# Attention in units of two head pairs, group 0's a\*b by attention segment, batch 1 inside the weight fold

## The chip, the core and the metric

The kernel runs on one core of one Trainium2 chip. The metric is device time in microseconds (us) of one execution, as a median over runs.

## The reference

Sliding-window causal attention over 8 batches, 8 heads, 576 positions and head size 64 (each query sees itself and the 63 positions before it), followed by a multiplicative feed-forward over the 4608 tokens of width 512:

```python
scores = scale * np.matmul(q, k.transpose(0, 1, 3, 2))
mask = (rel >= 0) & (rel < 64)
attn = exp(where(mask, scores, -1e9) - max); attn = attn / (sum(attn) + 1e-9)
x = np.matmul(attn, v)          # transposed to (4608 tokens, 512)
h = (x @ w1) * (x @ w2) @ w3    # w1, w2: 512 x 1024; w3: 1024 x 1024
out = h @ w_out                 # w_out: 1024 x 512
```

## The kernel before, in words

**Numbers.** Everything is multiplied in fp16 with fp32 sums. `w3 @ w_out` is folded on the chip into one matrix `wc_sb` (1024 x 512), so that a group of tokens costs `a`, `b`, their product, and one matmul with `wc_sb`.

**Attention units.** A batch has 12 units: 3 segments of 192 queries (`SEGS`) times 4 head pairs `j`. `scores(u)` (L251) computes the scores of one head pair with two matmuls into one PSUM tile `s_ps`, takes `exp` on ACT (L264) and zeroes what lies outside the window by two `affine_select` on POOL for each group of columns (L271, L273; segment 0 has two groups, so four of them). `values(u)` (L277) multiplies with v, whose tile carries columns of ones, so that four matmuls give the output and the row sums in `o_ps`; the division is two `Ln` of the sums (L298, L299), one `exp` of minus that (L301) and two DVE multiplies into the ring `xT` (L304, L305). `s_ps` and `o_ps` have two buffers of one PSUM bank each.

**Loads.** `load_qk` brings one batch of k or q into a tile of the four-buffer pool `stage`; `cast_qk` makes fp16 halves of it; `transposes` turns six 128x128 blocks on PE into `tp` (or into a buffer of `f_ps` while `early`) and copies them to `kT` or `qT`. `load_v` is a POOL-issued DMA that casts on the way; `copy_v` (L222) makes the two shifted v blocks on DVE. The weights come through `stage` too (`load_w12`, `load_wo`, `load_w3`), and are cast by DVE or POOL.

**Feed-forward.** 9 groups of 512 tokens. `ffn_ab(g, fc)` does 8 matmuls of 512 columns into two of the three `f_ps` buffers, an ACT copy (L379) and a DVE multiply (L380). `ffn_o(g, t)` does 8 matmuls, a DVE copy (L388) and, later, a store. `fold_t(fc)` turns a row block of w3 by 8 transposes (L432) and a DVE copy (L434); `fold_mm(fc)` does 8 matmuls (L440) and an ACT copy (L441).

**Order.** The order is written out by hand; each engine executes its own instructions in that order. First comes batch 0: loads, casts, transposes, then its 12 units alone, with filler matmuls on PE (`keep_busy`, L459) between them. Then a list of `slots`: 8 `ffn_ab` of group 0 with the casts and transposes of batch 1 hung on them (`todo`, L549), 8 fold steps, 4 `ffn_o`; from there on each group is 8 `ffn_ab` and 4 `ffn_o`. Each slot has a due time in units (L566 to L568), and after a slot `tick(u)` runs the units that are due: `scores(u)`, `values(u - LAG)` with `LAG = 2`, and the loads, casts and transposes for later batches (`late`, `second`). The units of batch 1 run one after each fold step and each of the first `ffn_o`.

Of the kernel before, what the change touches and what calls it, by code (L numbers as in the profile page):

```python
# [11 lines left out]
ALU = mybir.AluOpType  # L12
# [132 lines left out]
def kernel(  # L145
# [21 lines left out]
    RING = 4 * S  # L167

# [12 lines left out]
    ps_s = fast.enter_context(tc.tile_pool(name="ps_s", bufs=2, space=PSUM))  # L181
    ps_v = fast.enter_context(tc.tile_pool(name="ps_v", bufs=2, space=PSUM))
# [68 lines left out]
    def scores(u):  # L251
        b, r = divmod(u, 12)
        si, j = divmod(r, NJ)
        kT, qT = kTs[b], qTs[b % 2]
        seg = SEGS[si]
        w = sum(blk[2] for blk in seg)
        s_ps = ps_s.tile([P, 512], FP32, name="s_ps")
        c0 = 0
        for (k0, q0, n, _) in seg:
            nc.tensor.matmul(s_ps[:, c0:c0 + 2 * n].rearrange("k (a n) -> k a n", a=2), kT[:, j, k0:k0 + P],  # L260
                             qT[:, j, :, q0:q0 + n], start=True, stop=True, skip_group_check=True)
            c0 += 2 * n
        pt = sb.tile([P, 512], FP16, name="pt", bufs=4)
        nc.scalar.activation(pt[:, 0:2 * w], s_ps[:, 0:2 * w], AF.Exp, bias=-SHIFT, scale=scale)  # L264

        c0 = 0
        groups = [(0, 256, 128, 0, 0), (256, 384, 64, 64, 0)] if si == 0 else [(0, 512, 128, 64, -64)]
        for (lo, hi, n, off, step) in groups:
            sl = pt[:, lo:hi]
            nb = (hi - lo) // (2 * n)  # L270
            nc.gpsimd.affine_select(out=sl, in_=sl, pattern=[[step, nb], [0, 2], [1, n]], compare_op=ALU.is_ge,  # L271
                                    fill=0.0, base=off, channel_multiplier=-1)
            nc.gpsimd.affine_select(out=sl, in_=sl, pattern=[[-step, nb], [0, 2], [-1, n]], compare_op=ALU.is_ge,  # L273
                                    fill=0.0, base=63 - off, channel_multiplier=1)
        probs[u] = pt

    def values(u):  # L277
        b, r = divmod(u, 12)
        si, j = divmod(r, NJ)
        v16 = v16s[b % 2]  # L280
        pt = probs.pop(u)
        seg = SEGS[si]
        q_base = seg[0][1]
        o_ps = ps_v.tile([P, 2, 192], FP32, name="o_ps")
        first = True
        for a in range(2):
            c0 = 0
            for bi, (k0, q0, n, _) in enumerate(seg):
                nc.tensor.matmul(o_ps[:, a, q0 - q_base:q0 - q_base + n],  # L289
                                 v16[:, si * 2 + bi, j, a * D:a * D + P],  # L290
                                 pt[:, c0 + a * n:c0 + a * n + n],
                                 start=first, stop=(bi == 1), skip_group_check=True)
                first = False
                c0 += 2 * n
# [10 lines left out]
        nc.vector.tensor_tensor(xs[D:P], o_ps[D:P, 1, :], r[D:P], ALU.mult)  # L305

    NU = 12 * B
    LAG = 2
    VLOADS = {3: 0, 4: 2, 5: 3, 6: 4, 7: 5}

    def keep_sums(n):
# [5 lines left out]
    late = {5: [("load", 2, "q"), ("v", 1, 3)],  # L317
# [3 lines left out]
            9: [("copy", 1, 1), ("cast", 2, "k", 1)], 11: [("copy", 1, 4)]}  # L321
    second = {3: [("v", 1, 0)], 4: [("v", 1, 2)], 5: [("v", 1, 3)], 6: [("v", 1, 4)],
# [19 lines left out]

    def tick(u):

        b, r = divmod(u, 12)
        if u < NU:
            scores(u)
        ev = [] if b == 0 else (second if b == 1 else late).get(r, [])
# [15 lines left out]
    def ffn_ab(g, fc):  # L364
        if fc == 0:
            abs_[g] = sb.tile([P, 8, GT], FP16, name="ab", bufs=3)
        ab = abs_[g]
        a_ps = ps_f.tile([P, GT], FP32, name="f_ps")
        b_ps = ps_f.tile([P, GT], FP32, name="f_ps")
        x0 = g * GT % RING  # L370
        cuts = [(0, GT)] if x0 + GT <= RING else [(0, RING - x0), (RING - x0, GT)]
        for w, d in ((w1_sb, a_ps), (w2_sb, b_ps)):
            for dc in range(4):
                for ci, (lo, hi) in enumerate(cuts):
                    xc = (x0 + lo) % RING
# [82 lines left out]

# [13 lines left out]
    vl = list(VLOADS.values())  # L472
    for i, v16 in enumerate(v16s):
        nc.gpsimd.memset(v16.rearrange("p c j (a e) -> p (c j a) e", a=2)[:, :, D:2 * D], 1.0)
        if i == 0:
            load_v(0, vl[0])
    wst = [load_w12(moe_w1, 0), load_w12(moe_w2, 0)]
    keep_busy(45)
    for which in "kq":
        cast_qk(0, which, 0, dve_cp)  # L480
        cast_qk(0, which, 1, act_cp if which == "k" else pool_cp)
        for c in range(3):
# [139 lines left out]
```

## Time and profile before

| what | value |
|---|---|
| time, median of 3 runs | 339.63 us (338.09 to 339.88) |
| the profiled execution, its own time | 336.5 us |
| span of the profiled execution | 334.8 us |
| busy: PE, DVE, ACT, POOL | 287.5, 216.5, 211.9, 207.4 us |
| mean granted TensorE clock | 0.958 |

The shares of the whole span hide that the kernel has stages with different limits. The stages as they are used below: up to 26.5 us the first loads, until the first `values`; up to 64.5 us attention of batch 0, group 0's `ffn_ab` and batch 1's transposes; up to 114.25 us the weight fold with attention of batch 1 and group 0's `ffn_o`; up to 299 us groups 1 to 7 with the rest of the attention; then the last group.

### The profile page before, as it was taken

Reading aid. Unit: us, or ns where it says so; the run is one execution under the profiler, and the core shown is the slowest. Engines: PE = TensorE matmul, PEld = TensorE weight load, DVE = VectorE, ACT = ScalarE, POOL = GpSimd, SP = SyncE. Lnnn points to the kernel's source line nnn. Section 1 sums busy time; section 2 is a strip of 40 time slices with the busy share of each in tenths; the row PEclk is TensorE's granted clock in tenths of the full one; section 3 lists DMA queues with packets and bytes.
Section 4 is the critical chain, followed back from the end, with each engine's and each line's share of the span. In section 5 each row is a group of like instructions: output and inputs, shape, how many; then the busy total and the mean of one; then the engine's idle time right before and its main releaser. Section 6 shows DMA issues by size and latency. Waiting matters only on the chain.

```text
span 334.8 us, 6342 instructions
## 1 busy us (share of the span) xinstructions
PE 287.5 (86%) x2119; PEld 173.3 (52%) x2119; DVE 216.5 (65%) x395; ACT 211.9 (63%) x493; POOL 207.4 (62%) x341
## 2 busy tenths in 40 slices
PE   5727589669766999999999999999999999997890
PEld 5716555335433555555655679655555555543340
DVE  5424758924446966797898787768977866565230
ACT  1427873457625678698898877579879977732100
POOL 8454982759955757679978955778897564300000
PEclk9786989999979999999999999999999999999597
DMA  6992889983910395568857853196077020030011
GB/s 190 364 294 8 215 124 282 413 360 42 297 18 31 114 289 34 112 201 148 120 164 184 80 143 105 25 229 89 3 131 70 0 96 33 3 114 15 2 72 65
DMA packets 52203, 44.18 MB, mean 132 GB/s; under 512 B 39312, under 2 KB 39312, under 8 KB 52160
## 3 DMA queue, kind: packets, MB, share of 16 engines
q1 hardware_dynamic: 14656, 38.95, 33.5%
q0 software_dynamic: 37504, 4.72, 22.8%
q8 instruction: 19, 0.31, 0.4%
q14 instruction: 24, 0.20, 0.2%
HBM read 38.80 MB, written 9.44 MB: 144 GB/s over the span
## 4 chain that ended last, share of the span: by engine, by line
PE 67%; DVE 9%; POOL 9%; DMA 6%; issue 3%; ACT 3%; SPq 1%; DVEq 0%; POOLq 0%; ACTq 0%
PE f_ps L376 34%; PE f_ps L386 18%; PE o_ps L289 5%; PE s_ps L260 4%; PE tp L238 4%; DMA v<-in_v_dram 4%; POOL pt L273 3%; POOL pt L271 2%; DMA stage<-in_q_dram 2%; DVE qT L247 2%; POOL v L220 1%; PE f_ps L440 1%; DVE ab L380 1%; SPq L204 1%; POOL xT L425 1%
## 5 line engine op out<-in xcount | busy, mean ns | idle before, releaser
L376 PE MATMUL f_ps<-xT,w_sb 128*128 128x512 f16 (+1 forms) x640 | 136.5, 363 | 2.1 <-DVE xT L305 0.8
L271 POOL TENSOR_SCALAR_AFFINE_SELECT pt<-pt 128x512 f16<-128x512 f16 (+2 forms) x128 | 64.1, 500 | 60.1 <-ACT pt L264 59.5
L376 PEld LDWEIGHTS <-w_sb 128*128 128x128 f16 x640 | 60.8, 99 | 55.2 <-issue 6.6
L264 ACT ACTIVATE pt<-s_ps 128x512 f16<-128x512 f32 (+1 forms) x96 | 53.8, 561 | 26.3 <-PE s_ps L260 21.7
L273 POOL TENSOR_SCALAR_AFFINE_SELECT pt<-pt 128x512 f16<-128x512 f16 (+2 forms) x128 | 64.9, 507 | 8.7
L304 DVE TENSOR_TENSOR xT<-o_ps,r 64x192 f16<-64x192 f32 x96 | 33.4, 348 | 52.5 <-ACT r L301 50.5
L386 PE MATMUL f_ps<-wc_sb,ab 128*128 128x512 f16 x288 | 67.1, 379 | 0.0
L380 DVE TENSOR_TENSOR ab<-f_ps,a_sb 128x512 f16<-128x512 f32 x72 | 49.6, 691 | 21.1 <-PE f_ps L376 19.6
L379 ACT COPY a_sb<-f_ps 128x512 f32<-128x512 f32 x72 | 41.3, 573 | 29.4 <-PE f_ps L376 29.1
L289 PE MATMUL o_ps<-pt,v 128*128 128x128 f16 (+1 forms) x384 | 37.0, 219 | 12.6 <-DVE v L226 5.8
L298 ACT ACTIVATE ln_s<-o_ps 64x192 f32<-64x192 f32 x96 | 31.4, 327 | 18.6 <-PE o_ps L289 16.5
L386 PEld LDWEIGHTS <-ab 128*128 128x128 f16 x288 | 26.7, 98 | 27.1
L260 PE MATMUL s_ps<-qT,kT 128*128 128x256 f16 x192 | 35.5, 268 | 2.6 <-DVE qT L247 1.9
L301 ACT ACTIVATE r<-ln_s 128x192 f32<-128x192 f32 x96 | 34.8, 363 | 3.0
L289 PEld LDWEIGHTS <-v 128*128 128x128 f16 x384 | 27.3, 100 | 16.5 <-DVE v L226 6.4
L305 DVE TENSOR_TENSOR xT<-o_ps,r 64x192 f16<-64x192 f32 x96 | 34.6, 361 | 1.3
L220 POOL DMA_DIRECT2D v<-in_v_dram x40 | 34.3, 859 | 1.7 <-DVE xT L305 0.9
L299 ACT ACTIVATE ln_s<-o_ps 64x192 f32<-64x192 f32 x96 | 30.9, 322 | 1.1
L260 PEld LDWEIGHTS <-kT 128*128 128x128 f16 x192 | 18.5, 99 | 21.0 <-issue 3.1
L388 DVE COPY t2k<-f_ps 128x512 f32<-128x512 f32 x36 | 24.9, 692 | 6.6 <-PE f_ps L386 5.6
L247 DVE COPY qT<-tp 64x768 f16<-64x768 f16 x21 | 20.2, 961 | 6.3 <-ACT qT L247 6.0
L242 DVE COPY kT<-tp 128x768 f16<-128x768 f16 x21 | 19.9, 949 | 5.7 <-PE tp L238 5.7
(53 smaller groups left out, 227.2 us busy)
## 6 DMA issues: line engine op xcount, KB each, us to landing
stage<-in_k_dram SPq DMA_DIRECT2D x32, 288.0 KB
stage<-in_q_dram SPq DMA_DIRECT2D x32, 288.0 KB
out_dram<-t2k SPq DMA_DIRECT2D x36, 256.0 KB
stage<-in_moe_w_dram SPq DMA_DIRECT2D x8, 1024.0 KB
v<-in_v_dram POOLq DMA_DIRECT2D x32, 128.0 KB, 4.2
stage<-in_moe_w_out_dram SPq DMA_DIRECT2D x2, 1024.0 KB
v<-in_v_dram POOLq DMA_DIRECT2D x8, 64.0 KB, 3.3
lnsum<-ln_s SPq DMA_DIRECT2D x24, 6.0 KB
```

What stands on the lines that cost most here:

```text
L220: nc.gpsimd.dma_start(out=vh[lo:P, c], in_=v[b, :, s0:s0 + P - lo, :].rearrange("h s d -> s h d"))
L260: nc.tensor.matmul(s_ps[:, c0:c0 + 2 * n].rearrange("k (a n) -> k a n", a=2), kT[:, j, k0:k0 + P], qT[:, j, :, q0:q0 + n], start=True, sto ...
L264: nc.scalar.activation(pt[:, 0:2 * w], s_ps[:, 0:2 * w], AF.Exp, bias=-SHIFT, scale=scale)
L271: nc.gpsimd.affine_select(out=sl, in_=sl, pattern=[[step, nb], [0, 2], [1, n]], compare_op=ALU.is_ge, fill=0.0, base=off, channel_multipli ...
L273: nc.gpsimd.affine_select(out=sl, in_=sl, pattern=[[-step, nb], [0, 2], [-1, n]], compare_op=ALU.is_ge, fill=0.0, base=63 - off, channel_m ...
L289: nc.tensor.matmul(o_ps[:, a, q0 - q_base:q0 - q_base + n], v16[:, si * 2 + bi, j, a * D:a * D + P], pt[:, c0 + a * n:c0 + a * n + n], sta ...
L301: nc.scalar.activation(r, y[:, j], AF.Exp, scale=-1.0)
L305: nc.vector.tensor_tensor(xs[D:P], o_ps[D:P, 1, :], r[D:P], ALU.mult)
L376: nc.tensor.matmul(d[:, lo:hi], w[:, dc, fc * P:(fc + 1) * P], xT[:, dc, xc:xc + hi - lo], start=(dc == 0 and ci == 0), stop=(dc == 3), sk ...
L379: act_cp(a_sb, a_ps)
L380: nc.vector.tensor_tensor(ab[:, fc, :], b_ps, a_sb, ALU.mult)
L386: nc.tensor.matmul(o_ps, ab[:, fc, t * P:t * P + P], wc_sb[:, fc, :], start=(fc == 0), stop=(fc == 7))
```

## The change

- `scores(d)` and `values(d)` treat two head pairs at once: `s_ps` and `o_ps` become two banks wide, with one buffer each instead of two; one `exp` of 1024 (768 in segment 0) columns, one pair of masks, `Ln`, `exp` and multiplies over 384 columns a row instead of 192. The matmuls stay the same.
- In `tick(u)` an even u runs `scores(u // 2)`, an odd one `values(u // 2 - 1)`; `LAG` is 3; batch 0 and batch 1 no longer go through `tick`.
- The loads of batch 0's v wait on POOL for a copy from the first k tile (`gate`) and are then issued one after the other; batch 0's k and q are cast in thirds on DVE and ACT.
- Group 0's a\*b is done in pieces of 192, 192 and 128 tokens (`nf` blocks of `fc` share a PSUM tile) between the units of batch 0.
- Batch 1's casts, transposes and six units stand between the fold steps; batch 2's k transposes, its q and k casts and its v loads between those and `ffn_o(0, t)`.
- From group 1 on the slots are as before, but the first three slots of group 1 have no ticks, and carry batch 2's q transposes and batch 3's k casts.

The core of the diff:

```diff
-    ps_s = fast.enter_context(tc.tile_pool(name="ps_s", bufs=2, space=PSUM))
-    ps_v = fast.enter_context(tc.tile_pool(name="ps_v", bufs=2, space=PSUM))
+    ps_s = fast.enter_context(tc.tile_pool(name="ps_s", bufs=1, space=PSUM))
+    ps_v = fast.enter_context(tc.tile_pool(name="ps_v", bufs=1, space=PSUM))
+        s_ps = ps_s.tile([P, 2, 512], FP32, name="s_ps")
...
+        nc.scalar.activation(pt[:, :, 0:w], s_ps[:, :, 0:w], AF.Exp, bias=-SHIFT, scale=scale)
...
+        o_ps = ps_v.tile([P, 2, 512], FP32, name="o_ps")
...
+        y = lns[b, si][:, j0:j0 + 2]
+        nc.scalar.activation(y[0:D], o_ps[D:P, :, 0:192], AF.Ln)
+        nc.scalar.activation(y[D:P], o_ps[0:D, :, 192:384], AF.Ln)
+        nc.scalar.activation(r, y, AF.Exp, scale=-1.0)
...
+        nc.vector.tensor_tensor(xs[0:D], o_ps[0:D, :, 0:192], r[0:D], ALU.mult)
+        nc.vector.tensor_tensor(xs[D:P], o_ps[D:P, :, 192:384], r[D:P], ALU.mult)
...
+    LAG = 3
...
+        if u % 2 == 0 and d < ND:
+            scores(d)
...
+        if u % 2 == 1 and 12 <= d - 1 < ND:
+            values(d - 1)
...
+    gate = const.tile([1, 1], FP32)
+    pool_cp(gate, raws["k", 0][0:1, 0, 0:1])
+    for c in (0, 2, 3, 4, 5):
+        load_v(0, c)
...
+    scores(0)
+    scores(1)
+    copy_v(0, 1)
+    values(0)
+    keep_busy(8)
+    scores(2)
+    values(1)
+    cast_w12(0, 0, dve_cp)
+    cast_w12(1, 0, dve_cp)
+    keep_busy(8)
+    scores(3)
...
+    ffn_ab(0, 0, 2, 0, 192)
+    values(2)
+    scores(4)
+    copy_v(0, 4)
+    ffn_ab(0, 2, 2, 0, 192)
+    values(3)
+    cast_w12(0, 1, dve_cp)
+    scores(5)
+    ffn_ab(0, 0, 2, 192, 384)
+    cast_w12(1, 1, dve_cp)
+    values(4)
...
+    ffn_ab(0, 2, 2, 192, 384)
...
+    for fc in (4, 6):
+        ffn_ab(0, fc, 2, 0, 192)
+    values(5)
+    for fc in (4, 6):
+        ffn_ab(0, fc, 2, 192, 384)
+    cast_w3(0, stg["3", 0], dve_cp)
+    ffn_ab(0, 0, 4, 384, 512)
+    cast_w3(1, stg["3", 1], pool_cp)
...
+    ffn_ab(0, 4, 4, 384, 512)
...
+    for fc in range(3):
+        fold_step(fc)
+        cast_third(1, "k", fc, act_cp)
+    for c in range(3):
+        cast_third(1, "q", c, act_cp if c != 1 else dve_cp)
+        transposes(1, "k", c, early=True)
...
+    cast_w3(2, stg["3", 2], dve_cp)
+    fold_step(3)
+    for c in range(3):
+        transposes(1, "q", c, early=True)
+    copy_v(1, 1)
+    scores(6)
+    cast_w3(3, stg["3", 3], pool_cp)
+    fold_step(4)
+    scores(7)
+    values(6)
+    copy_v(1, 4)
+    fold_step(5)
+    scores(8)
+    values(7)
+    cast_qk(2, "k", 0, pool_cp)
+    fold_step(6)
+    scores(9)
+    values(8)
+    cast_qk(2, "k", 1, pool_cp)
+    fold_step(7)
+    scores(10)
+    values(9)
+    ffn_o(0, 0)
+    cast_qk(2, "q", 0, pool_cp)
+    scores(11)
+    transposes(2, "k", 0)
+    values(10)
...
+    ffn_o(0, 2)
+    values(11)
...
+    ffn_o(0, 3)
...
+    for g in range(1, NG):
...
+        first = 3 if g == 1 else 0
```

## Rows read from the trace of the kernel before

**Rows 1.** Busy time by stage: window, its length, then each engine's busy us, PEclk, DMA.
```profile
0.00:26.50 26.50, 13.02 (x144) 12.01 (x144) 10.79 (x13) 6.92 (x9) 15.90 (x26) 0.88 1.13 270
26.50:64.50 38.00, 30.41 (x262) 20.61 (x263) 26.09 (x44) 25.14 (x57) 25.18 (x31) 0.91 0.78 202
64.50:114.25 49.75, 36.26 (x294) 21.88 (x292) 25.83 (x49) 26.90 (x63) 35.99 (x59) 0.97 0.56 153
114.25:299.00 184.75, 183.88 (x1330) 108.81 (x1328) 141.88 (x272) 148.23 (x357) 130.36 (x226) 1.00 0.53 109
299.00:334.80 35.80, 23.93 (x99) 9.99 (x97) 11.95 (x20) 4.68 (x8) 0.00 (x0) 0.85 0.13 46
```
**Rows 2.** What PE waited for, 26.5 to 114.25 us: total us, times, longest.
```profile
PE o_ps L289 <- DVE v L226: 5.8, 1, 5.8
...
PE tp L238 <- POOL k L213: 3.5, 1, 3.5
```
**Rows 3.** The chain of waits at the start: start us, length us, what.
```profile
5.51 7.01 DMA stage<-in_q_dram
...
14.35 11.79 DMA v<-in_v_dram
...
26.52 0.40 PE o_ps L289 x3
```
**Rows 4.** DMA queues, 6 to 12, 12 to 18 and 18 to 22 us: packets, MB, share.
```profile
q0 software_dynamic: 1040, 0.13, 34.2%
...
q1 hardware_dynamic: 1183, 2.36, 104.7%
...
q0 software_dynamic: 494, 0.06, 24.0%
```
**Rows 5.** Costliest groups by shape: line, engine, shapes, count, busy us, mean ns of one.
```profile
L264 ACT ACTIVATE pt<-s_ps 128x512 f16<-128x512 f32 x64 | 38.2, 596 | 17.1 <-PE s_ps L260 13.7 <-POOL pt L273 2.1 <-POOL pt L271 0.4
...
L264 ACT ACTIVATE pt<-s_ps 128x384 f16<-128x384 f32 x32 | 15.6, 490 | 9.2 <-PE s_ps L260 8.0 <-POOL pt L273 0.5
...
L271 POOL TENSOR_SCALAR_AFFINE_SELECT pt<-pt 128x512 f16<-128x512 f16 x64 | 41.6, 650 | 35.8 <-ACT pt L264 35.2
...
L271 POOL TENSOR_SCALAR_AFFINE_SELECT pt<-pt 128x256 f16<-128x256 f16 x32 | 13.1, 410 | 24.3 <-ACT pt L264 24.3
...
L298 ACT ACTIVATE ln_s<-o_ps 64x192 f32<-64x192 f32 x96 | 31.4, 327 | 18.6 <-PE o_ps L289 16.5
...
L301 ACT ACTIVATE r<-ln_s 128x192 f32<-128x192 f32 x96 | 34.8, 363 | 3.0
...
L304 DVE TENSOR_TENSOR xT<-o_ps,r 64x192 f16<-64x192 f32 x96 | 33.4, 348 | 52.5 <-ACT r L301 50.5
...
L380 DVE TENSOR_TENSOR ab<-f_ps,a_sb 128x512 f16<-128x512 f32 x72 | 49.6, 691 | 21.1 <-PE f_ps L376 19.6
...
L213 POOL CAST k<-stage 128x1152 f16<-128x1152 f32 x13 | 14.9, 1148 | 0.0
```
**Rows 6.** The timeline: batch 0's q transposes, first scores, and a weight cast on DVE.
```profile
14.46 1.18 PE L238 MATMUL f_ps<-ident,q 128*128 128x128 f16 x18 [1.13 <-POOL q L213]
...
18.61 0.33 PE L260 MATMUL s_ps<-qT,kT 128*128 128x256 f16 x2 [1.85 <-DVE qT L247]
...
32.24 1.48 DVE L494 CAST w_sb<-stage 128x2048 f16<-128x2048 f32 x1
```
**Rows 7.** The chain of waits later: PE's pieces back to back, start us, length us.
```profile
56.11 0.34 PE tp L238 x6
...
285.32 0.22 PE s_ps L260 x2
285.54 0.22 PE o_ps L289 x4
285.77 1.73 PE f_ps L376 x8
```
**Rows 8.** Stretches after PE had waited: columns as in rows 1.
```profile
95.90:98.60 2.70, 2.70 (x9) 1.01 (x7) 1.43 (x3) 1.01 (x3) 0.89 (x1) 0.52 0.02 6
```

More of the change, by code (lines that the diff above doesn't have):

```diff
@@ L249, with scores @@
     probs, lns = {}, {}
-    def scores(u):
-        b, r = divmod(u, 12)
-        si, j = divmod(r, NJ)
+    def scores(d):
+        b, r = divmod(d, 6)
+        si, jp = divmod(r, 2)
         kT, qT = kTs[b], qTs[b % 2]
         seg = SEGS[si]
[L256 to L269, printed above, removed]
-            nb = (hi - lo) // (2 * n)
-            nc.gpsimd.affine_select(out=sl, in_=sl, pattern=[[step, nb], [0, 2], [1, n]], compare_op=ALU.is_ge,
+        w = 2 * sum(blk[2] for blk in seg)
+        s_ps = ps_s.tile([P, 2, 512], FP32, name="s_ps")
+        for jj in range(2):
+            c0 = 0
+            for (k0, q0, n, _) in seg:
+                nc.tensor.matmul(s_ps[:, jj, c0:c0 + 2 * n].rearrange("k (a n) -> k a n", a=2),
+                                 kT[:, 2 * jp + jj, k0:k0 + P], qT[:, 2 * jp + jj, :, q0:q0 + n],
+                                 start=True, stop=True, skip_group_check=True)
+                c0 += 2 * n
+        pt = sb.tile([P, 2, 512], FP16, name="pt", bufs=3)
+        nc.scalar.activation(pt[:, :, 0:w], s_ps[:, :, 0:w], AF.Exp, bias=-SHIFT, scale=scale)
+        for (lo, hi, n, off, step) in [(0, 256, 128, 0, 0), (256, 384, 64, 64, 0)] if si == 0 else [(0, 512, 128, 64, -64)]:
+            nb = (hi - lo) // (2 * n)
+            sl = pt[:, :, lo:hi]
+            if nb == 1:
+                pat = [[0, 2], [0, 2], [1, n]]
+            else:
+                pat = [[0, 2], [step, nb], [0, 2], [1, n]]
+            nc.gpsimd.affine_select(out=sl, in_=sl, pattern=pat, compare_op=ALU.is_ge,
@@ L280, in values @@
+    def values(d):
+        b, r = divmod(d, 6)
+        si, jp = divmod(r, 2)
+        j0 = 2 * jp
         v16 = v16s[b % 2]
-        pt = probs.pop(u)
+        pt = probs.pop(d)
         seg = SEGS[si]
         q_base = seg[0][1]
[L284 to L294, printed above, removed]
@@ L305, in values @@
[L305 to L309, printed above, removed]
+        o_ps = ps_v.tile([P, 2, 512], FP32, name="o_ps")
+        for jj in range(2):
+            first = True
+            for a in range(2):
+                c0 = 0
+                for bi, (k0, q0, n, _) in enumerate(seg):
+                    o0 = a * 192 + q0 - q_base
+                    nc.tensor.matmul(o_ps[:, jj, o0:o0 + n],
+                                     v16[:, si * 2 + bi, j0 + jj, a * D:a * D + P],
+                                     pt[:, jj, c0 + a * n:c0 + a * n + n],
+                                     start=first, stop=(bi == 1), skip_group_check=True)
+                    first = False
+                    c0 += 2 * n
@@ L471 @@
         nc.vector.memset(qT[0:D, :, 1, :], 0.0)
[L472 to L477, printed above, removed]
-    keep_busy(45)
[L479 to L482, printed above, removed]
-            transposes(0, which, c, early=True)
-        keep_busy(20)
@@ new lines, with cast_w12 @@
+    cast_third(0, "q", 0, dve_cp)
+    cast_third(0, "q", 1, act_cp)
+    cast_third(0, "q", 2, dve_cp)
+    for c in range(3):
+        transposes(0, "q", c, early=True)
+    keep_busy(25)
+    for i, w in enumerate((moe_w1, moe_w2)):
+        wst[i, 1] = load_w12(w, 1)
+    def cast_w12(i, half, cp):
+        cp(w12[i][:, :, half * 512:half * 512 + 512], wst[i, half])
+    w3Ts, stg = {}, {}
+    scores(0)
[5 more added lines that the diff above has]
+    values(1)
@@ L564 @@
+    for g in range(1, NG):
+        part = [lambda g=g, fc=fc: ffn_ab(g, fc) for fc in range(8)] + \
+               [lambda g=g, t=t: ffn_o(g, t) for t in range(4)]
         lo = need[g]
         hi = need[g + 1] if g + 1 < NG else NU
+        first = 3 if g == 1 else 0
         for i, w in enumerate(part):
```

194 lines of the change are left out of this document (92 added, 102 removed), and 13 rows, old and new, of tables (late, second).

## The prediction, as it was recorded before the change was run

> **What bounds the kernel now.** I read the busy time by stage first. Groups 1 to 7 are bound by TensorE: 183.88 of 184.75 us busy at a granted clock of 1.00 [rows 1], so DVE, ACT and POOL time saved there buys nothing. What the kernel can lose is ahead of 114.25 us: 26.5 us until the first `values`, then 38.0 and 49.75 us in which PE is busy 30.4 and 36.3 us, part of it filler at a lowered clock [rows 1]. PE's waits name the causes: v's shifted copy, 5.8 us, and batch 2's k casts on POOL, 3.5 us [rows 2]. The chain of waits says that the first of these is a transfer: v's second load was issued at 14.35 and took 11.79 us [rows 3].
>
> So the sum goes by four stages: the first `values` (V), the start of the fold (F), the start of group 1 (G), and what follows, 184.75 + 35.8 us now [rows 1].
>
> **Prices of paired instructions.** An operation on twice the columns pays its fixed cost once. From two shapes of one kind [rows 5]: `exp` 596 ns at 512 and 490 at 384, so 0.83 ns a column and 1.02 us at 1024 (0.81 at 768); a mask 650 at 512 and 410 at 256, so 1.13 us at 1024, hence 2.26 for the two masks of a pair; `Ln` from 327 ns to 0.49 and the division's `exp` from 363 to 0.52, by the slope of `exp`; a DVE multiply from 348 to 0.55 (slope from 691 ns at 512). Over 48 pairs this takes some 33 us from ACT, 23 from POOL, 15 from DVE. Their worth is in the stages before G alone.
>
> With `o_ps` in one buffer, `values(n+1)` waits for the multiplies of `values(n)`: matmuls 0.4, two `Ln` 0.97, `exp` 0.52, two multiplies 1.1, and some 0.3 of hops, together 3.3 us, which I call a turn.
>
> **V, now 26.5.** v's loads are now issued behind a gate that the first k transfer opens, instead of at 14.35. When it opens the trace doesn't show; I bound it by 5 us (PE idles for k; a quarter of k is in) and 8 (all of k). The software queue moved 1040 packets in 6 to 12 us beside q, none in 12 to 18 with the weights in the hardware queue (v's loads were issued from 14.35 on), and 494 in 18 to 22 [rows 4]. The two loads that the first `values` needs are 2048 packets. From a gate at 5 most of them go before 12 and they land near 20; from 8 near 24; if the weights starve them again, at 26. The scores come first: q lands at 12.5 [rows 3]; casting in thirds without POOL's cast costs 0.6 before the transposes, which take 4.15 us to the first scores [rows 6], so 17.3; `exp` and four masks (0.65 twice, 0.41 twice) bring V to 20.8 at the earliest. I take 22.5, between; ends 20.8 and 26.5. The Trainium skill (DMA: Bandwidth & Descriptors, section Queues, rings and completion order) says that each DMA engine takes turns between the queues at packet granularity. By that rule V is 20.8 and the sum 1.7 us less; the empty software queue of 12 to 18 us speaks against it.
>
> **V to F, now 38.0.** Counting from V: `values(1)` at 3.4, its multiplies end at 6.6. On DVE two w1/w2 casts stand behind them, 1.48 each [rows 6], to 9.6; the first piece of a\*b waits for them and holds up `values(2)`, queued behind it on PE, until 10.4. One turn gives `values(3)` at 13.7. The next piece needs its multiplies, at 17.0, so `values(4)` comes at 18.5; on DVE its multiplies stand behind two more casts and end at 21.7. PE does the pieces of fc 2 to 6 (1.3 us each, from 1.73 for 512 columns [rows 7]) until 23.7; `values(5)`, its multiplies 27.0; the last two pieces 1.9 each: 31.3. All PE filler is gone, and a\*b, 13.8 us, hides in the turns. This replaces 38.0, which also held batch 1's transposes.
>
> **F to G, now 49.75.** From F: three fold steps of 2.2 (1.73 and 8 transposes of 0.06) after a first copy, 7.9. Batch 1's k transposes and copies, then a w3 cast of 1.4 behind them on DVE: fold step 3 ends at 14.7, with 2.5 us of PE idle. The q transposes, in PE's queue ahead of `scores(6)`, cost 4.15 again [rows 6]: 18.8. `scores(6)`, its masks to 22.4, and on POOL the last w3 cast of 2.1 (two of 1024 columns, by the k cast's 1148 ns for 1152 [rows 5]) to 24.5, for which fold step 5 waits. From there POOL sets the pace: five more pairs of masks, 2.26 each, and three casts of 1.15 [rows 5] between them, end at 41.1; `values(11)`, the rest of `ffn_o`, one turn: group 1 can start at 45.3. The loads of w3, k and q of batches 1 and 2 are issued 10 us and more ahead of use, so they cost nothing here; v's loads for batch 1 stand behind the wo casts on POOL and land some 10 us before the copies. If the hardware queue is late by more than that, F to G grows by as much.
>
> **Clock and coupling.** PE now idles for 2.5 to 5 us in five places. After the 3.5 us wait in front of 93.4 the granted clock stood at 0.52 for 2.7 us [rows 2, 8], the 1.2 GHz level, costing 1.4 us. A few such pieces on the path, and turns that meet a busy ACT or POOL, cost between 0 and 10 us; I take 4, since about three of the pieces lie on the path.
>
> G is then 22.5 + 31.3 + 45.3 + 4 = 103.1, against 114.25: 11.15 us earlier.
>
> **After G, now 220.55.** Some work moved past G: scores of three units and values of one (0.22 each), five sets of transposes (0.34 each) [rows 7]: 2.5 us of PE. The first three slots of group 1 run no ticks, so after the fourth four ticks are due at once: `values(12)` is queued behind `scores(12)` and `scores(13)` and waits for `exp` and four masks, 2.2 us of PE idle, which also holds up all `ffn_ab` behind it. In the steady part two ticks with two slots take 4.6 us against a turn of 3.3, and ACT has `exp` 1.02, a copy and a qT copy ahead of the `Ln`; slack about 1 us; I add 1 us. The last group and its check keep their order: 0. Together +5.7.
>
> Span 334.8 - 11.15 + 5.7 = 329.4; with the 1.7 us around the span (336.5) 331.1. The median of the runs stands 3.1 above the profiled execution, so the forecast is 334.2.
>
> **The rivals.**
> - *The early stages run as added up, or better.* No clock loss (-4), V at 20.8 (-1.7), the burst hidden (-2.2), no steady loss (-1): down to 325; middle 328. For it: the paired operations leave every engine more slack than before.
> - *v is late again.* The weights still hold the software queue: V = 26.5, and the coupling at 5 instead of 4: 339. For it: no packet in 12 to 18 us [rows 4].
> - *Batch 1 doesn't really run inside the fold.* POOL (masks, w3 and k casts, v issues) and the w3 casts keep fold steps waiting; F to G stays near 49.75 plus the transposes it now holds, some 53: 342.
> - *Slower: one PSUM buffer each for `s_ps` and `o_ps`.* In groups 1 to 7 PE is full; if a turn overruns its 4.6 us because ACT is behind, every pair stops PE. With 36 pairs, each 0.1 us a pair is 3.6 us; above 0.2 us a pair the gain of 5.4 is gone, at 0.3 the time is 345. Against it: slack of about 1 us. The Trainium skill (Perfetto Trace Analysis, section Optimizing Tensor Performance) has independent matmul groups rotate through PSUM banks so that emptying one overlaps the next; by it this is what the change gives up. The kernel before, with two buffers, shows no stall of the kind, so no row decides it.
>
> **How the numbers follow.** Forecast 0.41; better 0.22; v late 0.14; fold not overlapped 0.11; PSUM turns 0.12. Half a per cent, about what a measurement of this kernel can tell from no change, is 1.7 us: faster is under 337.9. The forecast's own range is 330 to 338, so faster takes nearly all of it, the better case and a little of v: 0.66; same, most of v late and a part of the fold case and of the forecast's edge: 0.16; slower, the PSUM case and the rest: 0.18. The range, 325 to 343, takes in the ends of V (-1.7, +4) and of the coupling (-4, +6).
>
> **What would show it.** First `values` near 22 us; fold transposes (`fold_t`) near 55; first `ffn_ab` of group 1 near 103, followed after 7 us by one PE gap of about 2 us; PE over 98% busy in groups 1 to 7; POOL masks at about 1.13 us. The forecast is wrong if v's loads still end the first wait at 26, if PE waits for `xT` multiplies or for `exp` recur in the steady part, or if PE runs long at the 1.2 GHz level before G.

## The result and the profile after

The changed kernel takes 326.97 us (median of 4, 325.52 to 328.72), the kernel before 338.86 (median of 4, 335.19 to 339.88) beside it: a ratio of 0.967, 95% interval 0.9581 to 0.976. The forecast was 334.2, range 325 to 343. A kernel's executions fall into a faster and a slower state and differ widely (13 of the kernel before on one chip span 331.67 to 339.01), so the ratios compare fast ones alone, while the medians of before take in all.

The profiled execution took 328.72 us with a span of 327.0. Its stages, cut at the first matmul of `values`, the first `fold_t`, the first `ffn_ab` of group 1 and the first of group 8 (window, length, busy us of PE, PEld, DVE, ACT, POOL, granted clock, DMA):

```profile
0.00:21.58 21.58, 12.34 (x129) 11.31 (x130) 13.98 (x15) 7.58 (x9) 12.06 (x17) 0.84 1.05 270
21.58:55.88 34.30, 26.55 (x273) 23.55 (x273) 21.40 (x28) 17.48 (x32) 23.26 (x21) 0.75 0.69 229
55.88:100.47 44.59, 35.79 (x287) 21.42 (x286) 23.31 (x37) 25.45 (x41) 24.68 (x29) 0.96 0.67 132
100.47:291.11 190.64, 187.58 (x1368) 111.17 (x1367) 136.85 (x209) 129.85 (x218) 122.29 (x143) 1.00 0.58 120
291.11:327.00 35.89, 23.79 (x98) 9.88 (x96) 11.64 (x19) 4.69 (x8) 0.00 (x0) 0.84 0.13 48
```

The 26.5 us of [rows 1] are not the first matmul of `values`, which stood at 20.47 in the kernel before; they are where the rest of that first unit came, behind its wait for v. By this cut V is 22.45 in after and V to F 33.43; the table and the text take it from here on, unless they say that the first matmul is meant.

| stage | before | forecast | after |
|---|---|---|---|
| to V | 26.50 | 22.5 | 22.45 |
| V to F | 38.00 | 31.3, and 4 of coupling in one of the three | 33.43 |
| F to G | 49.75 | 45.3 | 44.59 |
| groups 1 to 7 | 184.75 | 190.45 | 190.64 |
| last group | 35.80 | 35.8 | 35.89 |
| span | 334.8 | 329.4 | 327.0 |

G comes 13.8 us earlier, and 6.0 us of that is given back behind it. Of the 7.2 us between forecast and median, 2.4 lie in the sum of stages.

Prices of the pair, by shape (engine, shapes, count, busy us, mean ns of one), against [rows 5]: `exp` 1022 and 810 ns, masks 1151 and 1170, `Ln` 487, the division's `exp` 522, a multiply 549. The prediction had 1.02 and 0.81 us, 1.13, 0.49, 0.52 and 0.55.

```profile
L287 POOL TENSOR_SCALAR_AFFINE_SELECT pt<-pt 128x1024 f16<-128x1024 f16 x32 | 37.4, 1170 | 2.2
L285 POOL TENSOR_SCALAR_AFFINE_SELECT pt<-pt 128x1024 f16<-128x1024 f16 x32 | 36.8, 1151 | 39.1 <-ACT pt L276 38.9
L276 ACT ACTIVATE pt<-s_ps 128x1024 f16<-128x1024 f32 x32 | 32.7, 1022 | 14.9 <-PE s_ps L271 14.0 <-POOL pt L287 0.7 <-POOL q L215 0.2
L321 DVE TENSOR_TENSOR xT<-o_ps,r 64x384 f16<-64x384 f32 x48 | 26.4, 549 | 55.4 <-ACT r L318 53.9 <-POOL pt L285 1.5
L318 ACT ACTIVATE r<-ln_s 128x384 f32<-128x384 f32 x48 | 25.1, 522 | 1.5
L315 ACT ACTIVATE ln_s<-o_ps 64x384 f32<-64x384 f32 x48 | 23.4, 487 | 36.7 <-PE o_ps L306 36.5
```

The first `values` no longer waits for v. The timeline (start, length, engine, line, what, idle before) of the kernel before has the wait for v inside that unit; the one of after has v's two shifted copies done at 19.4, and PE waiting for the masks twice:

```profile
20.47 0.22 PE L289 MATMUL o_ps<-pt,v 128*128 128x128 f16 x1 [0.26 <-POOL pt L273]
26.52 0.40 PE L289 MATMUL o_ps<-pt,v 128*128 128x64 f16 x3 [5.83 <-DVE v L226]
...
18.76 0.29 DVE L234 COPY v<-v 64x512 f16<-64x512 f16 x1
19.08 0.29 DVE L236 COPY v<-v 64x512 f16<-64x512 f16 x1
...
21.58 0.22 PE L306 MATMUL o_ps<-pt,v 128*128 128x128 f16 x1 [0.92 <-POOL pt L287]
22.45 0.69 PE L306 MATMUL o_ps<-pt,v 128*128 128x64 f16 x7 [0.65 <-POOL pt L287]
```

What PE waited for from V to F (first three rows), from F to G (two) and from G to the end (three): total us, times, longest.

```profile
PE f_ps L392 <- DVE w_sb L520: 2.9, 2, 2.3
PE f_ps L392 <- DVE xT L322: 2.2, 1, 2.2
PE o_ps L306 <- POOL pt L287: 1.6, 2, 0.9
...
PE s_ps L271 <- DVE qT L257: 2.9, 1, 2.9
PE f_ps L451 <- DVE xT L444: 1.7, 1, 1.7
...
PE tp L474 <- DVE ones L472: 3.5, 1, 3.5
PE tp L248 <- POOL k L215: 1.5, 1, 1.5
PE tp L248 <- DVE kT L252: 0.7, 1, 0.7
```

They are the waits that the prediction had worked out: w1/w2 casts in front of the first piece of a\*b, the next piece's multiplies, q transposes ahead of `scores(6)` and a w3 cast behind k copies. In groups 1 to 7 no wait for the division's multiplies is left, and only one short one for `exp` or masks.

### The profile page after: what moved, and what is told of

It reads as the page before. It is cut to its first block, busy times and chain, and to the rows that moved or that the text cites. A ratio compares the mean times of both kernels' runs of the same rounds, so it can differ in the third digit from the quotient of the medians.

```text
span 327.0 us, 5827 instructions
## 1 busy us (share of the span) xinstructions
PE 286.1 (87%) x2151; PEld 177.3 (54%) x2151; DVE 207.2 (63%) x307; ACT 185.1 (57%) x308; POOL 182.3 (56%) x207
## 4 chain that ended last, share of the span: by engine, by line
PE 67%; DVE 10%; ACT 6%; DMA 6%; issue 4%; POOL 3%; SPq 1%; DVEq 0%; ACTq 0%; POOLq 0%
PE f_ps L392 33%; PE f_ps L405 16%; PE o_ps L306 6%; PE s_ps L271 5%; DMA stage<-in_k_dram 4%; PE f_ps L459 3%; PE tp L248 3%; DMA stage<-in_q_dram 2%; DVE qT L257 2%; DVE xT L322 2%; ACT ln_s L316 1%; ACT r L318 1%; ACT pt L276 1%; DVE k L222 1%; DVE w_sb L520 1%
## 5 line engine op out<-in xcount | busy, mean ns | idle before, releaser
L392 PE MATMUL f_ps<-xT,w_sb 128*128 128x512 f16 (+3 forms) x768 | 140.4, 335 | 5.2 <-DVE w_sb L520 2.9
L392 PEld LDWEIGHTS <-w_sb 128*128 128x128 f16 x768 | 71.2, 101 | 53.1 <-issue 6.7
L285 POOL TENSOR_SCALAR_AFFINE_SELECT pt<-pt 128x512 f16<-128x512 f16 (+1 forms) x64 | 53.7, 839 | 83.0 <-ACT pt L276 82.8
L398 DVE TENSOR_TENSOR ab<-f_ps,a_sb 128x512 f16<-128x512 f32 (+1 forms) x74 | 49.8, 676 | 22.0 <-PE f_ps L392 19.8
L397 ACT COPY a_sb<-f_ps 128x512 f32<-128x512 f32 (+1 forms) x74 | 41.9, 567 | 36.2 <-PE f_ps L392 35.6
L321 DVE TENSOR_TENSOR xT<-o_ps,r 64x384 f16<-64x384 f32 x48 | 26.4, 549 | 55.4 <-ACT r L318 53.9
L276 ACT ACTIVATE pt<-s_ps 128x1024 f16<-128x1024 f32 (+1 forms) x48 | 45.7, 951 | 24.6 <-PE s_ps L271 23.1
L287 POOL TENSOR_SCALAR_AFFINE_SELECT pt<-pt 128x512 f16<-128x512 f16 (+1 forms) x64 | 54.3, 849 | 4.4
L315 ACT ACTIVATE ln_s<-o_ps 64x384 f32<-64x384 f32 x48 | 23.4, 487 | 36.7 <-PE o_ps L306 36.5
L306 PE MATMUL o_ps<-pt,v 128*128 128x128 f16 (+1 forms) x384 | 29.7, 221 | 6.1 <-POOL pt L287 2.7
L322 DVE TENSOR_TENSOR xT<-o_ps,r 64x384 f16<-64x384 f32 x48 | 26.9, 561 | 0.7
L318 ACT ACTIVATE r<-ln_s 128x384 f32<-128x384 f32 x48 | 25.1, 522 | 1.5
L316 ACT ACTIVATE ln_s<-o_ps 64x384 f32<-64x384 f32 x48 | 23.1, 482 | 0.6
L257 DVE COPY qT<-tp 64x768 f16<-64x768 f16 x18 | 17.3, 961 | 7.8 <-ACT qT L257 7.6
```

Of the source, the lines that this page charges most:

```text
L276: nc.scalar.activation(pt[:, :, 0:w], s_ps[:, :, 0:w], AF.Exp, bias=-SHIFT, scale=scale)
L285: nc.gpsimd.affine_select(out=sl, in_=sl, pattern=pat, compare_op=ALU.is_ge, fill=0.0, base=off, channel_multiplier=-1)
L287: nc.gpsimd.affine_select(out=sl, in_=sl, pattern=[[-s, m] for s, m in pat], compare_op=ALU.is_ge, fill=0.0, base=63 - off, channel_multip ...
L306: nc.tensor.matmul(o_ps[:, jj, o0:o0 + n], v16[:, si * 2 + bi, j0 + jj, a * D:a * D + P], pt[:, jj, c0 + a * n:c0 + a * n + n], start=firs ...
L318: nc.scalar.activation(r, y, AF.Exp, scale=-1.0)
L322: nc.vector.tensor_tensor(xs[D:P], o_ps[D:P, :, 192:384], r[D:P], ALU.mult)
```

## Experiments

**Both kernels once more, on another chip.** `before_again` and `after_again` are the two kernels unchanged.

> The kernel before once more, for a second trace. Its four runs lay between 335.2 and 339.9 us, and the trace that the prediction read (336.5) was one of the faster ones. If the spread is in the first loads (v behind the weights), the stage up to the first values differs by 2 to 4 us from 26.5 and the stretch of groups 1 to 7 stays at 184.8 within 0.3. The rival: the spread is in the clock, and then the stages with a lowered granted clock differ.

> The changed kernel once more, for the interval and a second trace. Expected 0.965 of the kernel before, 325 to 329 us, stages within 1 us of the first trace (first values at 21.6, fold at 55.9, group 1 at 100.5, 190.6 for groups 1 to 7).

Before 335.9 us (13 runs, 331.67 to 339.01; the profiled one 334.28); after 326.32 (4 runs, 324.44 to 328.03), ratio 0.9723 (0.9637 to 0.9809). Stages of before: 25.90, 37.65, 51.00, 184.93, 33.02; of after: 22.48, 32.87, 43.17, 193.22, 34.46. So a stage before G is repeated within 1.5 us, the last group differs by 2.8 us between two executions of before, and groups 1 to 7 by 2.6 between two of after (within 1 us was expected). In before V differs by 0.6 and groups 1 to 7 by 0.2, while the granted clock was 0.85 and 0.92 in the last group and 0.97 and 0.90 from F to G: the spread goes with the clock, as the rival had it. In after, the wait for batch 3's first k cast was 4.1 us instead of 1.5.

**One part alone.** `pair_only` is the kernel before with the units of two head pairs, one PSUM buffer each of twice the size, in the old order; `order_only` is the kernel after with its units done as two single ones, and two buffers each for `s_ps` and `o_ps` again:

```diff
# pair_only, against before
-    ps_s = fast.enter_context(tc.tile_pool(name="ps_s", bufs=2, space=PSUM))
+    ps_s = fast.enter_context(tc.tile_pool(name="ps_s", bufs=1, space=PSUM))
...
-        s_ps = ps_s.tile([P, 512], FP32, name="s_ps")
+        s_ps = ps_s.tile([P, 2, 512], FP32, name="s_ps")
...
-        if u < NU:
-            scores(u)
+        d = u // 2
+        if u % 2 == 0 and d < ND:
+            scores(d)
# order_only, against after
+    def scores(d):
...
+            scores_u(2 * d + jj)
+
+    def values(d):
+        for jj in range(2):
+            values_u(2 * d + jj)
```

> The paired units alone (one exp, one set of masks, one division for two head pairs, one buffer each for s_ps and o_ps, LAG 3) in the order of the kernel before. If the gain comes from the order of the early stages, this is worth little: 335 to 341 us, since groups 1 to 7 are full on PE and the first batch is bound by turns of 3.3 us for two pairs against 1.57 us for one before. If it comes from the fewer and longer instructions, at least half of the gain is here: 328 to 333.

> The changed kernel with unpaired units inside: each scores and values of two head pairs is two of the old ones, with two buffers each for s_ps and o_ps; the new order stays. If the order makes the gain, 326 to 331 us (masks of a pair 2.6 instead of 2.26 us on POOL, six pairs between fold and group 1: some 2 us more there). If the pairing makes it, 333 or more.

`pair_only`: 337.81 us, ratio 1.0073 (1.0011 to 1.0135), stages 25.89, 37.99, 49.62, 185.40, 33.50. `order_only`: 329.70, ratio 0.9838 (0.9758 to 0.9918), stages 21.43, 33.25, 44.30, 194.61, 34.91. Pairing without the order gives nothing; the order without pairing gives 6.2 us of the 9.6 (by the ratios 1.6 of 2.8%). Which piece of the order brings how much was tried for v's issue only, below. Its early stages are as short as after's: the time saved on ACT, POOL and DVE bought nothing ahead of G. The medians of `order_only` and after lie 3.4 us apart; in the profiled executions `order_only` is 1.8 to 3.0 us longer behind G. Its windows of 12 us there show the clock (columns as above):

```profile
98.98:110.98 12.00, 9.25 (x61) 4.69 (x60) 8.70 (x14) 5.63 (x9) 4.08 (x5) 1.00 1.29 277
110.98:122.98 12.00, 11.16 (x72) 6.42 (x70) 6.50 (x12) 7.38 (x19) 11.14 (x23) 0.72 0.77 213
```

**v late in the new order, v early in the old.** `v_late` issues v's first load with no gate and the other four behind q's cast; `before_vgate` issues all five behind the gate that the change brings:

```diff
# v_late, against after
-    pool_cp(gate, raws["k", 0][0:1, 0, 0:1])
-    for c in (0, 2, 3, 4, 5):
-        load_v(0, c)
+    load_v(0, 0)
...
+    pool_cp(gate, q16s[0][0:1, 12, 0:1])
+    for c in (2, 3, 4, 5):
+        load_v(0, c)
# before_vgate, against before
-            load_v(0, vl[0])
+            gate = const.tile([1, 1], FP32)
+            pool_cp(gate, raws["k", 0][0:1, 0, 0:1])
+            for c in vl:
+                load_v(0, c)
...
-    for c in vl[1:]:
-        load_v(0, c)
```

> The changed kernel with batch 0's v issued as in the kernel before: the first load at once, the other four only when q has been cast (near 15 us). If v's early issue is what brings the first values from 26.5 to 21.6, they move back to 25.5 to 27 and the time rises by 4 to 5 us over the changed kernel (ratio 0.985). If the scores and masks would have set that moment anyway, or the weights now come sooner and the weight casts catch up, the rise is under 1.5 us.

> The kernel before with only the new issue of batch 0's v: all five loads on POOL behind the gate on k, ahead of the second memset. If the first wait is worth its whole length, first values at 21 to 22 and 4 to 5 us less (ratio 0.987). If the next wait is late instead (weights that share the queues with v, ACT-bound units), 0 to 2 us less.

`v_late`: 330.65 us, ratio 0.9784 (0.9731 to 0.9838), against 0.9723 and 0.967 for after; V at 25.05, V to F 33.74, F to G 45.56. PE's waits have v again:

```profile
PE o_ps L306 <- DVE v L236: 4.2, 1, 4.2
```

`before_vgate`: 334.18, ratio 0.9924 (0.9875 to 0.9973), beside 336.63 for before. V fell from 26.5 to 21.03, 5.5 us, and V to F stayed at 37.95; F to G, 52.03 at a granted clock of 0.87, and the last group, 36.11, took part of it back in that execution. In the new order v's 2.6 us of V go with 0.006 to 0.011 of the ratio, 2 to 4 us, in intervals that overlap; in the old one 5.5 us of V brought 2.4. Each time that is between the two cases: the wait counts, but not in full.

**The clock ahead of G.** `filler` is the kernel after with 62 filler matmuls (its expectation counts 72):

```diff
     copy_v(0, 1)
+    keep_busy(10)
     values(0)
     keep_busy(8)
     scores(2)
+    keep_busy(10)
     values(1)
...
     scores(3)
+    keep_busy(22)
...
     scores(5)
+    keep_busy(20)
     ffn_ab(0, 0, 2, 192, 384)
```

> The changed kernel with 72 more filler matmuls in four places between the first scores and the third piece of a*b, where PE idles. The stage from first values to fold stood at a granted clock of 0.75 (first trace) and 0.85 (second) and took 34.3 and 33.7 us against 31.3 added up. If the clock is the difference, the granted clock rises over 0.9, the stage falls to 31 to 32 and the time by 2 to 3 us; if turns and weight casts set it, the stage stays within 1 us.

327.09 us, ratio 0.9679 (0.9618 to 0.9739): no gain. The row of V to F shows the clock up and the stage as long:

```profile
21.70:55.27 33.57, 26.38 (x324) 24.01 (x324) 22.05 (x28) 17.27 (x32) 20.76 (x18) 0.90 0.70 216
```

At 0.75, 0.85 and 0.90 the stage took 34.30, 33.74 and 33.57 us, all counted from the first matmul of `values`. The filler takes time on PE itself, so this run alone would leave room for a gain of the clock; but `improved1`, below, has the stage shorter than any of them at a clock of 0.77. Turns and casts set it.

From F to G the length goes with the clock. Two executions of the same code there, with the same waits for the w3 cast and the q transposes, of `after_again` and of `after_split` (below):

```profile
55.35:98.52 43.17, 34.36 (x287) 20.77 (x286) 23.27 (x37) 25.47 (x41) 25.59 (x30) 1.00 0.74 147
55.99:101.55 45.56, 37.37 (x289) 22.03 (x287) 23.04 (x37) 25.57 (x41) 24.63 (x29) 0.93 0.69 135
```

After's own 44.59 came at 0.96, `filler`'s 43.15 at 1.00, and 45.56 in `v_late` at 0.93: up to 2.4 us between executions of one code.

**The waits taken away.** `improved1` does five things in the kernel after: POOL's second memset goes behind k's casts, one w1 cast behind the first division, two w3 casts and batch 1's q transposes ahead, and batch 3's loads of k and q from behind group 0's stores to where batch 2's are issued:

```diff
-    ones_of(1)
...
+    pool_cp(gate_k, k16s[0][0:1, 12, 0:1])
+    ones_of(1)
...
     values(0)
+    cast_w12(0, 0, dve_cp)
...
     values(1)
-    cast_w12(0, 0, dve_cp)
...
+    cast_w3(2, stg["3", 2], dve_cp)
     for c in range(3):
         cast_third(1, "q", c, act_cp if c != 1 else dve_cp)
         transposes(1, "k", c, early=True)
     load_qk(2, "k")
     load_qk(2, "q")
+    load_qk(3, "k")
...
-    cast_w3(2, stg["3", 2], dve_cp)
-    fold_step(3)
+    cast_w3(3, stg["3", 3], pool_cp)
     for c in range(3):
         transposes(1, "q", c, early=True)
+    fold_step(3)
     copy_v(1, 1)
     scores(6)
-    cast_w3(3, stg["3", 3], pool_cp)
+    load_qk(3, "q")
...
```

> The changed kernel with the waits that its trace names moved: POOL's second memset behind the k casts (they ran 3.9 instead of 1.0 us beside it: 1 us), the first w1 cast behind the first division instead of the second (1.8), the third w3 cast ahead of batch 1's k copies (1.7), batch 1's q transposes ahead of fold step 3 instead of behind it (2.9), the last w3 cast ahead of the first masks, batch 3's k and q loads ahead of the first stores (0.3 to 3). If each wait goes and nothing takes its place, 8 us less than the changed kernel (318); if the next wait is late in each place, 2 to 4 us less.

320.89 us, ratio 0.9481 (0.9419 to 0.9543). Stages 23.67, 31.25, 40.53, 189.67, 34.78. The median is 5.4 to 6.1 us under after's two, between the two cases. V to F, 33.43 and 32.87 in after, is now 31.25. That it equals the 31.3 of the prediction is luck: one cast that the prediction had on the path is gone from it. F to G lies 4.8 below the prediction's term and 2.6 below `after_again`, which had the same clock of 1.00 there. In this execution v's second load landed at 23.3 behind the same gate, PE waited 3.0 us for it, and V was later than after's; why is open.

**Batch 3's loads alone.** `loads_ahead` moves those two loads in after, `order_loads` in `order_only`:

```diff
     load_qk(2, "q")
+    load_qk(3, "k")
...
     scores(6)
+    load_qk(3, "q")
...
     store()
-    load_qk(3, "k")
     load_v(2, 4)
     load_v(2, 5)
     ffn_o(0, 3)
     store()
-    load_qk(3, "q")
```

> The kernel after with the loads of batch 3's k and q issued ahead of scores 6 in the fold, in place of behind the stores of group 0. Theory (the prediction was wrong that loads cost nothing: these queue behind stores, POOL's k cast starts only at 109.2, TensorE waits 1.5 to 4.1 us for it at the start of group 1 and its clock is lower behind the wait): that wait is under 0.3 us, group 1 to group 8 takes 188.5 to 190.5 us in place of 190.6 and 193.2, and the median falls by 1.5 to 3 us to 323.5 to 325.5. Rival (the wait hides the one for POOL's masks behind it, which the prediction put at 2.2 us): the wait returns on the masks' rows as o_ps waiting for POOL, 1.5 to 2.5 us, group 1 to group 8 stays over 190.5, and the median is within 1 us of the kernel after.

> The new order with the unpaired units, as in the kernel that had the order alone, and with batch 3's loads of k and q issued ahead of scores 6. It tells what pairing adds in the new order (3.4 us between the medians, 329.7 against 326.3). Theory (pairing adds little of its own, and the order alone lost 3 to 4 us by the wait for batch 3's k and the low clock behind it): group 1 to group 8 falls from 194.6 to 189 to 191 us and the median to 324 to 326.5, within 1.5 us of the paired kernel with the same loads. Rival (pairing does its part in the steady groups too, by fewer instructions for ScalarE and POOL): group 1 to group 8 stays over 192.5 and the median stays 2.5 to 4 us above the paired kernel with the same loads.

In after, batch 3's k loads stand in SP's queue behind the stores, and POOL idles 7.6 us for them. The timeline of SP's queue, then POOL's casts by shape (the last column is idle time and what ended it), then PE:

```profile
94.04 5.27 SPq L414 DMA_DIRECT2D out_dram<-t2k  x3
99.36 2.67 SPq L206 DMA_DIRECT2D stage<-in_k_dram  x4
...
L215 POOL CAST k<-stage 128x1152 f16<-128x1152 f32 x12 | 13.7, 1150 | 7.6 <-DMA stage<-in_k_dram 7.6
...
111.52 0.51 PE L248 MATMUL tp<-ident,k 128*128 128x128 f16 x6 [1.52 <-POOL k L215]
```

`loads_ahead`: 325.88 us, ratio 0.9798 (0.9675 to 0.992); groups 1 to 7 189.50 and the wait for k gone; PE now waits for the masks there:

```profile
PE o_ps L306 <- POOL pt L287: 1.1, 2, 0.6
```

So the stage shortens by 1.1 to 3.7 us, as the theory had it, while the median is within 1.1 of after's, as the rival had it: in the profiled execution PE waited 1.35 us for v again, so that V came at 23.30, and F to G took 45.57 at the clock of 0.93, with the code there almost the same. F to G and groups 1 to 7 together took 235.07 us, and 235.2 to 236.4 in the five executions that have after's order there (after, `after_again`, `v_late`, `filler`, `after_split`): moving the loads took the wait away, but gained 1.3 us at most in that sum. `order_loads`: 327.74 us, ratio 0.9865 (0.9752 to 0.9978); groups 1 to 7 took 192.47, not the 189 to 191 expected. Its waits there are those of `loads_ahead`, but the clock fell again:

```profile
110.88:122.88 12.00, 11.30 (x73) 6.08 (x73) 6.74 (x14) 8.76 (x22) 11.33 (x21) 0.86 0.41 83
```

Pairing in the new order is thus worth 1.9 to 3.4 us (two pairs of medians; the runs of the second pair overlap), neither of the two cases, and the rows put it behind G. Whether it holds the clock up is not settled: that stretch was at 0.72 and 0.86 in the two unpaired kernels, at 0.86 in `after_again` and `filler`, and at 1.00 in the other paired ones.

**The check in the last group.** `after_split` leaves the five DVE instructions of the check where they are and lets PE's matmul that needs them come two slots later; `improved2` does the same in `improved1`:

```diff
             if quiet == 4:
                 check_sums()
+            if quiet == 6:
+                check_end()
```

> Only one thing differs from the kernel after: the check of the sums in the last group leaves its five VectorE instructions where they are, and TensorE's two small matmuls that wait for them come two slots (16 matmuls of 128x512) later. In the kernel after, TensorE waits 3.5 us for these five, and the 24 matmuls behind that wait take 8.07 us there and 6.67 us in the other profile of the same code, against 5.2 at full clock. Theory (the wait sets off a fall of the granted clock whose length changes from execution to execution, and this is a good part of the spread of the times): the wait is under 0.5 us, the last group takes 29 to 31 us in place of 34.5 to 35.9, the median is 320 to 323, and the runs of one call lie within 2 us. Rival (the spread comes from the early stages, and the clock falls in the last group in any case): the last group 31.5 to 33, the median 323 to 325, and the spread stays at 3 us and more.

> The improved kernel (second memset behind the k casts, one w1 cast behind the first division, w3 casts ahead of the k copies, batch 1's q transposes ahead of fold step 3, batch 3's loads early), which took 320.9 us, and in it the check of the sums with its two small matmuls two slots later. Theory: 3.5 us of wait and up to 2.8 us of half clock go from the last group, which takes 29 to 31 us in place of 34.8; the median is 314.5 to 317.5. Rival (the clock falls there in any case): the last group takes 31.5 to 33 us and the median is 317.5 to 319.5.

The timelines of PE from the check on, of `before_again`, after and `after_split` in turn:

```profile
311.58 0.19 PE L455 MATMUL tp<-ones,okv 48*1 48x1 f32 x2 [3.47 <-DVE ones L453]
311.70 5.35 PE L376 MATMUL f_ps<-xT,w_sb 128*128 128x512 f16 x24
...
303.21 0.19 PE L474 MATMUL tp<-ones,okv 48*1 48x1 f32 x2 [3.47 <-DVE ones L472]
303.32 8.14 PE L392 MATMUL f_ps<-xT,w_sb 128*128 128x512 f16 x24
...
304.46 0.18 PE L480 MATMUL tp<-ones,okv 48*1 48x1 f32 x2
304.57 1.90 PE L392 MATMUL f_ps<-xT,w_sb 128*128 128x512 f16 x8
```

The same wait of 3.5 us is followed by 24 matmuls that take 5.35 us in one execution and 8.14 in another (6.74 to 7.04 in six more). Without the wait the last group takes 29.91 us, as the theory had it, against 34.46 to 36.35 in the eight executions of the new order that have it. `after_split` takes 322.57 us (320.31 to 323.78), ratio 0.9686 (0.9553 to 0.9819): 4 us under after's medians on other chips and 3.3 under that of `loads_ahead` on the same one. The ratio is no lower than after's 0.967 and 0.9723, so the gain is read from the stage and not from it. The spread of its runs, 3.5 us, did not shrink; there the rival was right, for the early stages of after differ as well. `improved2` takes 314.26 us (313.78 to 315.11), ratio 0.9465 (0.9352 to 0.9577): by the ratio some 18 us under before, and by the medians 11.6 under `loads_ahead` on the same chip and some 12 under after on others (by the ratios 7 to 9). Its stages, cut at the first matmul of `values` (by the cut of the table 21.86 and 30.75):

```profile
0.00:21.00 21.00, 11.14 (x129) 10.39 (x130) 11.68 (x15) 7.59 (x9) 11.84 (x18) 0.92 1.04 267
21.00:52.61 31.61, 24.60 (x273) 22.24 (x272) 21.06 (x29) 17.48 (x32) 22.89 (x20) 0.84 0.78 253
52.61:93.05 40.44, 34.51 (x287) 20.73 (x286) 23.21 (x37) 25.34 (x41) 26.06 (x30) 1.00 0.96 205
93.05:282.55 189.50, 187.23 (x1367) 111.14 (x1366) 135.92 (x209) 129.87 (x218) 122.15 (x143) 1.00 0.55 108
282.55:312.20 29.65, 21.18 (x99) 9.31 (x97) 11.39 (x19) 4.69 (x8) 0.00 (x0) 0.94 0.16 58
```

Its runs lie within 1.3 us. That says nothing of the waits: those of `order_only`, which has them, lie within 0.9.

## Why the prediction came out as it did

**The direction and the stages were right.** Faster was given 0.66. The sum's span of 329.4 stands 2.4 above the 327.0 measured; V to F lies 2.1 above its term, every other stage within 1 us, and G came 1.4 us behind the sum of its three stages, where 4 were set aside for coupling. Most of its signs appeared: first `values` at 21.58 or 22.45 by the two cuts (near 22), `fold_t` at 55.88 (near 55), PE 98.4% busy in groups 1 to 7, masks at 1.15 and 1.17 us. Group 1 began at 100.47, not near 103, and the gap behind it, 1.5 us after 9.5, had another cause than the masks. One of the signs of being wrong came as well, PE long at the lower clock level before G (0.75 from V to F); `filler` and `improved1` show that this cost the stage little.

**The step that failed is the last one, from the profiled execution to the median.** The time fell by 11.9 us between the two medians, where 5.4 was forecast. I added 3.1 us because the median of before stood that far above its profile. The median of after stands 1.75 below its profile: 4.85 of the 7.2 us of the miss. Over the twelve series here with several runs each, the profiled execution lies between 3.65 below its median (`pair_only`) and 2.88 above it (`loads_ahead`). One such difference is a draw, not a property that the next kernel inherits; it belonged into the range. (The range's upper end, 343, is also 1.2 short of the two ends that it is said to take in, 334.2 + 4 + 6.)

**V: right value, partly by luck, and the doubt against it fell.** The term was 22.5, taken between 20.8 and 26.5; 22.45 came, set by the masks, as the lower end has it. The margin above that end was meant for v's loads. It was used up by the scores, at 18.78 and not 17.3: k's casts took 3.87 us beside POOL's memset (last section), and q's waited for DVE. The working had no such term. I had taken the software queue's empty stretch of 12 to 18 us [rows 4] for starvation. In after the two queues moved, in 12 to 18 us:

```profile
q1 hardware_dynamic: 915, 1.83, 89.8%
q0 software_dynamic: 1061, 0.13, 34.1%
```

About one packet each. The Trainium skill (DMA: Bandwidth & Descriptors, section Queues, rings and completion order) has each DMA engine take turns between its queues by packet; this trace agrees, and so does `before_vgate` with its V at 21.03. What kept the queue empty in the kernel before stays open; `v_late` shows it again, with loads issued from 13.98 on, no packet before 18, and then 600 beside 629 of the other queue until 22. That v is late again, the rival with 0.14, did not come in after's two executions. It isn't dead: behind the same gate v's second load held PE up in two of nine executions, for 3.0 us in `improved1` and 1.35 in `loads_ahead`. `v_late` shows 2 to 4 us for it, where I had put 4.8.

**V to F: 33.4 for 31.3.** The turns and waits are those of the working. The 2.1 us arise up to `values(3)`, which comes 15.7 us behind V and not 13.7: the first turn took 0.5 more, the pair of w1/w2 casts 0.3 (3.29 us, where two of 1.48 from [rows 6] were counted, beside masks on POOL), and the first piece of a\*b and the turn behind it the rest (8 matmuls of that piece took 1.46 us, later 16 took 1.51). From there on the lag stays between 1.7 and 2.7 us. `improved1` and `improved2`, where one of the two casts stands ahead, take 31.25 and 30.75. The 4 us of "clock and coupling" covered this; raising the clock alone, in `filler`, changed the stage by 0.2 to 0.7 us.

**F to G: 44.6 for 45.3.** The two waits named there, the w3 cast behind the copies and the q transposes ahead of `scores(6)`, are in the trace with 1.7 and 2.9 us. `improved2` takes both away and has 40.44, 2.7 less than `after_again` at the same clock. The first of POOL's masks and the last w3 cast end at 24.7 behind F (24.5 in the working). The sum from there is wrong in itself: 24.5 and five pairs of masks and three casts make 39.3, not 41.1; the trace has 40.4, with short waits between them. And 0 to 2.4 us of this stage go with the clock, which the prediction put into its term for coupling. The rival in which batch 1 doesn't fit inside the fold is dead.

**After G: the size was right by luck, the make-up partly wrong.** Forecast +5.7, measured 5.9 in groups 1 to 7 and 0.1 in the last (8.3 and 1.4 between the second executions of the two kernels). PE's busy time there rose by 3.7 us (I had 2.5 of moved work), its idle time by 2.2. That idle time was to be the masks behind the burst of ticks; it was PE waiting for batch 3's first k cast, late because batch 3's loads stand behind stores. There the sentence that loads of k and q cost nothing failed: I had followed batches 1 and 2 and not batch 3. Behind it the masks wait does come, 1.1 us, as `loads_ahead` shows. The 1 us for a steady loss was not needed: with no wait for multiplies in the steady part, and with PE busy for 185.35 of 185.40 us there in `pair_only`, the rival of one PSUM buffer each (0.12) is dead.

**What the prediction did not ask.** It priced pairing's savings as slack ahead of G and didn't ask what the order does without them. `order_only` has the same early stages: there the gain is that of the order.

## What to carry to other kernels

Price each stage by what ends its longest wait, and follow every moved load to the end of the queue it joins: here the order brought most of the gain, and the next 12 us by the medians (7 to 9 by the ratios) lay in six small moves, the largest a result that PE had asked for too early. Halving the instruction count on engines that don't bound a stage gave nothing by itself. Cut the stages of two traces at the same piece of work. Put the difference between a profile and a median into the range, not into the forecast.

## What the runs showed of the hardware

**DVE casts beside POOL's work.** In after the two k casts of 128x768 took 3.87 us while POOL's memset of 128x3072 ran, which took 3.03. With that memset moved, in `improved2`, the casts took 1.38 together and the memset 2.65. Timelines of after, then of `improved2`:

```profile
8.06 3.87 DVE L222 CAST k<-stage 128x768 f16<-128x768 f32 x2 [2.04 <-DMA stage<-in_k_dram]
8.47 3.03 POOL L495 MEMSET v<- 128x3072 f16 x1
...
8.01 1.38 DVE L222 CAST k<-stage 128x768 f16<-128x768 f32 x2 [1.99 <-DMA stage<-in_k_dram]
9.57 2.65 POOL L501 MEMSET v<- 128x3072 f16 x1
```

The Trainium skill (SBUF — State Buffer, section SBUF: two separate sides) says that VectorE in some of its modes and GpSimd share a pair of ports as an exclusive lock, and that the loser waits for the whole instruction. The rows fit that: the casts' extra 2.5 us are about the length of one memset. Masks and w1/w2 casts look the same: a mask of 128x1024 took 1.99 to 2.13 us beside such a cast and 1.11 without one, and two casts 3.29 us in after and 4.05 in `after_again`, against 1.23 each in `improved1`, where the masks beside them took the longer time. No run tried that alone.

**The clock after one and the same wait.** Behind the 3.5 us in the last group 24 matmuls took 5.35, 6.74 to 7.04 or 8.09 to 8.21 us, in executions of code that is the same there; [rows 8] shows the lower level, 0.52, behind another such wait. The Trainium skill (TensorE: Matmul & The Clock Gate, section Part 1: The HAM clock gate) says that the number of slow matmuls varies from run to run of one kernel; these rows agree, and put it at 0 to 2.9 us for a wait.
